# Attention into a two-layer network on one core: all loads as casting DMAs from GpSimd, values regrouped in bf16, one PSUM pool, a new plan

## The chip, the cores and the metric

The kernel runs on one core of one Trainium2 chip. The metric is the device time of one execution in microseconds (us). The core's engines work side by side, each from its own queue in program order: PE multiplies matrices, DVE (VectorE) and ACT (ScalarE) do elementwise work and empty PSUM, POOL (GpSimd) does elementwise work in SBUF, SP (SyncE) issues DMAs. A DMA issued from SP is written in hardware; one issued from POOL is written by POOL's own cores.

## The reference, cut to what matters

```python
# q, k, v: (8, 8, 576, 64) fp32, p: (8, 8, 32, 64) fp32; batch, heads, tokens, head size
p_packed = sm_attn(p, k, v)              # 32 packed queries over 576 tokens
out = sm_attn(q, p_packed, p_packed)     # 576 queries over 32 packed tokens
x = out.transpose(0, 2, 1, 3).reshape(4608, 512)
h = x @ w_in                             # 512 x 2048
r = np.maximum(h, 0.0)
return ((r * r) @ w_out).astype(np.float32)   # 2048 x 512
```

`sm_attn` is softmax attention with scale 1/8. The 4608 rows of x are 8 batches of 576 tokens.

## The kernel before, in words

Work goes by batch b, and in a batch by two groups qd of four heads. The steps of one batch, by the names that the planner gives them:

- Loads (L404 for k and q, L411 for v, issued from SP): fp32 tiles `kq_f` (pool of 4) and `v_f` (one tile), 576 KB for each of two k and two q, four pieces for v. The weights come as fp32 tiles `w_f` (6 of them), eight of 512 KB for `w_in` (L434) and eight for `w_out` (L443). All loads stand in one list on SP: batch 0, `w_in`, batch 1, `w_out`, batch 2 and so on, and the stores of the result (L651, four per 128 tokens) go through the same queue.
- Casts to bf16, `Ck`, `Cv`, `Cq`, `WI`, `WO` (all at the helper's line L349 on ACT and L351 on DVE or POOL). From batch 1 on, k, v and q are cast on POOL. Weights are cast on POOL or DVE. The cast of v also regroups it, from the order of heads to groups of 128 tokens.
- `Tk` and `Tq`: 32x32 block transposes on DVE (L468, L462).
- `X`: spreads the transposed p of a batch into a block-diagonal tile `pT_bd` (L351; POOL from batch 1 on).
- `S1` (L478, L492): p against k, and the exponential on ACT (L485, L499). `PV` (L513, L517): times v, and the sums.
- `XT`: takes the small products out of PSUM into `pq_bd` and `ppT`.
- `M` (L548): since the second attention's values are only 32 rows per head, they are multiplied into `w_in` first, so that the first layer has a folded weight `M` of 128 x 2048 per group, made in four chunks of 512 columns. L556 (ACT) and L558 (DVE) take it out of PSUM with the softmax factor.
- `S2`, `N` (L578 to L606): q against the packed products, exponential, and the normalisation (ln, exp of minus ln, product on DVE).
- `F1` (L618): 16 blocks of 128 columns of the first layer, each four matmuls of 288 columns, then relu on ACT (L626; for batch 0 DVE too, L628) and the square on DVE into `gT` (L633).
- `F2` (L642): 36 tiles of 128 tokens, each 16 matmuls of 512 columns, taken out by ACT or DVE into `o_sb` and stored.

The order on every engine is written by a planner (`Plan`, run when the program is built): each step has pieces with an engine and an assumed time in us, dependences, and slots that it takes and gives back. `forward` places, again and again, the piece that can start first, and the instructions are issued in the order of the planned starts. So each engine's queue has a fixed order, and an instruction whose input is late holds up all behind it on its engine. PSUM is split into three pools: `a` (2 banks, attention), `h` (2 pairs of banks: S2, N, F1), `o` (2 banks, F2).

Of the kernel before, what the change touches and what calls it, by code (L numbers as in the profile page):

```python
# [26 lines left out]
HOP = 0.2  # L27


class Piece:  # L30
    __slots__ = ("step", "stage", "k", "alts", "start", "end", "alt", "pred", "late", "order", "only")

    def __init__(self, step, stage, k, alts):
        self.step, self.stage, self.k, self.alts = step, stage, k, alts
        self.late = self.only = None
# [3 lines left out]

# [9 lines left out]
class Plan:  # L49
# [3 lines left out]
    def __init__(self, slots):  # L53
        self.nslots = slots
        self.streams, self.base = [], {}
        self.fill = 0
# [4 lines left out]
    def forward(self):  # L61

        busy = {e: ([-1.0], [t]) for e, t in self.base.items()}
        slots = {k: [] for k in self.nslots}
        last = {k: 0.0 for k in self.nslots}
# [5 lines left out]
        def ready(st, t):  # L71
            pred = []
            for d in st.deps:
                x = done.get(d)
                if x is None:
                    return INF, pred
                t = max(t, x[0] + HOP)
                pred.append(x)
            for p, n in st.take:
                s = slots[p]  # L80
                m = len(s) - self.nslots[p]
                for j in range(max(0, m), m + n):
                    x = s[j]
                    if x is None:
                        return INF, pred
                    t = max(t, x[0] + HOP)
                    pred.append(x)
                t = max(t, last[p])
            return t, pred

        def gap(e, us, t):

            s0, s1 = busy.setdefault(e, ([-1.0], [0.0]))
            i = bisect_right(s0, t) - 1
            t = max(t, s1[i])
            while i + 1 < len(s0) and s0[i + 1] < t + us - 1e-9:
                i += 1
                t = max(t, s1[i])
            return t, i
# [25 lines left out]
        while True:  # L125
            best = None
            for i, (prio, steps) in enumerate(self.streams):
# [3 lines left out]
                key = pc.late  # L131
                if best is not None and key is not None and key >= best[0]:
                    continue
                t, pred = ready(pc.step, since[i])
                if key is None:
                    key = greedy(pc, t) + 0.003 * prio
                if t < INF and (best is None or key < best[0]):
                    best = (key, pc, t, pred, i)
            for x in pend:
                key = x[0].late  # L140
                if key is None:
                    key = greedy(x[0], x[1]) + 0.003 * (x[2] - 0.5)
                if best is None or key < best[0]:
                    best = (key, x[0], x[1], x[3], x)
            if best is None:
                break
            _, pc, t, pred, src = best
            b = None
            for i, (e, us, _) in enumerate(pc.alts):
                if (pc.only is None or pc.only == i):  # L150
                    s = t if e == "-" else gap(e, us, t)[0]
                    if b is None or s + us < b[0]:
                        b = (s + us, s, i, e)
            f, s, a, e = b
            pc.start, pc.end, pc.alt, pc.pred = s, f, a, pred
# [4 lines left out]
            if pc.stage == 0:  # L160
# [3 lines left out]
                for p, k in st.take:  # L164
                    held[p, st.name] = range(len(slots[p]), len(slots[p]) + k)
                    slots[p] += [None] * k
                    last[p] = s
                ends = [pc]
            else:
                pend.remove(src)  # L170
                prio = src[2]
                ends = src[4]
                ends.append(pc)
                done[f"{st.name}/{pc.stage}.{pc.k}"] = (f, ((pc, 0.0),))
                if len(ends) < len(st.pieces[pc.stage]):
                    continue
            fin = max(p.end for p in ends)
            i = pc.stage
            lag = st.lag
            for p, taker in st.give_at[i]:  # L180
                x = (fin + lag, tuple((q, lag) for q in ends))
                for j in held.pop((p, taker)):
                    slots[p][j] = x
            if i + 1 < len(st.pieces):
                hop = 0.0 if e == "-" else HOP
                pr = [(fin + hop - HOP, tuple((q, hop - HOP) for q in ends))]
                state = []
                for q in st.pieces[i + 1]:
                    pend.append((q, fin + hop, prio, pr, state))
            else:  # L190
                done[st.name] = (fin + lag, tuple((q, lag) for q in ends))
        assert all(pos[i] == len(s) for i, (_, s) in enumerate(self.streams)) and not pend, [
            s[pos[i]].name for i, (_, s) in enumerate(self.streams) if pos[i] < len(s)]
        return out, max(p.end for p in out)

    def backward(self, out, T):
        late = {}
        busy = {}
        for pc in sorted(out, key=lambda p: (p.end, p.start), reverse=True):
            us = pc.end - pc.start  # L200
            lf = late.get(id(pc), T)
            e = pc.alts[pc.alt][0]
            if e != "-":
                iv = busy.setdefault(e, [])
                j = 0
                while j < len(iv) and iv[j][0] >= lf - 1e-9:
                    j += 1
                while j < len(iv) and iv[j][1] > lf - us + 1e-9:
                    lf = min(lf, iv[j][0])
                    j += 1  # L210
                s = lf - us
                if j > 0 and abs(iv[j - 1][0] - lf) < 1e-9:
                    iv[j - 1] = (s, iv[j - 1][1])
                    if j < len(iv) and abs(iv[j][1] - s) < 1e-9:
                        iv[j - 1] = (iv[j][0], iv[j - 1][1])
                        del iv[j]
                elif j < len(iv) and abs(iv[j][1] - s) < 1e-9:
                    iv[j] = (iv[j][0], lf)
                else:
                    iv.insert(j, (s, lf))  # L220
            else:
                s = lf - us
            pc.order = s
            for x in pc.pred:
                for q, lag in x[1]:
                    late[id(q)] = min(late.get(id(q), T), s - HOP - lag)
        for pc in out:
            pc.late = pc.order

    def score(self, out, T):  # L230
        pe = [p for p in out if p.alts[p.alt][0] == "PE"]
        return T + 0.2 * sum(p.start for p in pe) / len(pe)

    def first(self, rounds):
        best = None
        for r in range(rounds + 1):
            out, T = self.forward()
            v = self.score(out, T)
            if best is None or v < best[0]:
                best = (v, T, [(p, p.start, p.end, p.alt) for p in out])  # L240
            if r < rounds:
                self.backward(out, T)
        return best

    def settle(self, best):
        for p, s, f, a in best[2]:
            p.start, p.end, p.alt = s, f, a
            p.late, p.only = s, a if len(p.alts) > 1 else None

    def vary(self, best, seed):  # L250

        r = random.Random(seed)
        hor = best[1] if r.random() < 0.2 else 70.0
        c, w = r.random() * hor, 0.5 + 6.0 * r.random() ** 2
        p_key, p_alt, sig = r.random() ** 2, 0.6 * r.random() ** 2, 0.3 + 6.0 * r.random() ** 3
        for p, s, f, a in best[2]:
            if abs(s - c) < w:
                if r.random() < p_key:
                    p.late = s + sig * (2.0 * r.random() - 1.0)
                if len(p.alts) > 1 and r.random() < p_alt:  # L260
                    p.only = int(r.random() * len(p.alts))
        try:
            out, T = self.forward()
        except AssertionError:
            return None
        return self.score(out, T), T, [(p, p.start, p.end, p.alt) for p in out]

    def run(self, rounds=0, seeds=()):
        best = self.first(rounds)
        for s in seeds:  # L270
            self.settle(best)
            best = self.vary(best, s) or best
        self.log = []
        free = dict(self.base)
        for p, s, f, a in sorted(best[2], key=lambda x: x[1]):
            e, us, fn = p.alts[a]
            if e == "PE":
                self.fill = self.fills(s - free.get(e, 0.0), s)
            free[e] = f
            self.log.append((p.step.name, p.stage, e, s, f))  # L280
            fn()
        return best[1]
# [5 lines left out]
def kernel_impl(tc, q, k, v, p, w_in, w_out, out):  # L288
# [7 lines left out]
    NCB = DMODEL // P  # L296
    NWC = DFF // WCH
    HALF = S // 2
    JH = JT // 2
    TOK = B * S  # L300
    NW = 6
    NT = TOK // P

    with ExitStack() as ctx:
        ctx.enter_context(tc.manual_schedule())
        consts = ctx.enter_context(tc.tile_pool(name="consts", bufs=1))
        stg = ctx.enter_context(tc.tile_pool(name="stg", bufs=4))
        qkv = ctx.enter_context(tc.tile_pool(name="qkv", bufs=4))
        vpool = ctx.enter_context(tc.tile_pool(name="vpool", bufs=1))
        att = ctx.enter_context(tc.tile_pool(name="att", bufs=2))  # L310
        small = ctx.enter_context(tc.tile_pool(name="small", bufs=3))
        mpool = ctx.enter_context(tc.tile_pool(name="mpool", bufs=2))
        rpool = ctx.enter_context(tc.tile_pool(name="rpool", bufs=4))
        opool = ctx.enter_context(tc.tile_pool(name="opool", bufs=3))
        ps_att = ctx.enter_context(tc.tile_pool(name="ps_att", bufs=2, space=bass.MemoryType.PSUM))
# [584 lines left out]
```

## Time and profile before

| | us |
|---|---|
| runs | 269.36, 271.1, 274.66 |
| median of the 3 runs | 271.1 |
| span of the profiled execution, from its first to its last instruction | 272.6 |
| PE, DVE, ACT, POOL busy in it | 245.0, 169.6, 167.8, 80.1 |

The page has no time of the profiled execution other than its span. The span lies 1.5 us above the median of the runs and inside their range. PE's busy time counts matmuls with modelled ends, so a PE that waits between matmuls in a group can still be shown as busy; the number of matmuls in a stretch tells more. The page's section 2 gives the span in 40 slices of 6.8 us. The view by windows gives the same for chosen stretches, and the timeline the single instructions, with the idle time ahead of one and what ended it in brackets.

### The profile page before, as it was taken

To read this page: it belongs to the slowest core of one execution; us is meant where nothing else is said; L and a number is where in the kernel's file an instruction comes from. 1 tells how busy PE (TensorE), PEld (TensorE's weight loads), DVE (VectorE), ACT (ScalarE), POOL (GpSimd) and SP (SyncE) were. 2 spreads that over 40 slices of the span, in tenths; PEclk is the share of its full clock that TensorE was granted. 3 is DMA by queue.
4 is the path that set the end of the run, shared out by engine and by line. 5 is a ranking of instruction groups with operands and counts; after the bars stand their busy time and mean duration, and the time that the engine had idled before them with its cause. 6 is when DMAs were issued, how large, how long until landed. Compare 5 with 4: busy or idle time off the path is not lost.

```text
span 272.6 us, 5046 instructions
## 1 busy us (share of the span) xinstructions
PE 245.0 (90%) x1840; PEld 136.5 (50%) x1840; DVE 169.6 (62%) x327; ACT 167.8 (62%) x298; POOL 80.1 (29%) x99
## 2 busy tenths in 40 slices
PE   0558859999998889989999999999999999999993
PEld 0522533555664345745655665566446646644441
DVE  4658997999798498599687648963354504510000
ACT  3547735966786857778659776877657816831110
POOL 5242595592594831443170403000000000000000
PEclk9999995999999979999999999999999999999999
DMA  7999999965949994149328412110211122112222
GB/s 257 321 377 396 383 386 394 358 214 159 319 164 287 364 356 151 42 135 368 95 63 248 182 31 59 41 36 22 62 41 39 39 59 59 40 42 76 77 77 77
DMA packets 26744, 46.99 MB, mean 172 GB/s; under 512 B 5728, under 2 KB 13920, under 8 KB 26720
## 3 DMA queue, kind: packets, MB, share of 16 engines
q1 hardware_dynamic: 26192, 46.55, 51.6%
q8 instruction: 14, 0.23, 0.4%
q10 hardware_dynamic: 528, 0.13, 0.2%
q14 instruction: 10, 0.08, 0.1%
HBM read 37.22 MB, written 9.44 MB: 171 GB/s over the span
## 4 chain that ended last, share of the span: by engine, by line
PE 52%; DMA 18%; DVE 15%; SPq 5%; POOL 3%; issue 3%; ACT 2%; POOLq 0%; DVEq 0%
PE ps_o L642 29%; PE ps_h L618 15%; DVE gT L633 6%; DMA out_dram<-o_sb 5%; DMA w_f<-in_moe_w_in_dram 5%; DMA kq_f<-in_q_dram 5%; DMA v_f<-in_v_dram 4%; PE ps_a L548 3%; SPq L651 3%; DVE kT L468 3%; DVE M L558 2%; SPq L411 2%; PE ps_s L578 2%; ACT o_sb L349 1%; POOL v_b L351 1%
## 5 line engine op out<-in xcount | busy, mean ns | idle before, releaser
L642 PE MATMUL ps_o<-w_out_b,gT 128*128 128x512 bf16 x576 | 150.5, 383 | 0.5 <-DVE gT L633 0.4
L626 ACT ACTIVATE r<-ps_h 128x576 bf16<-128x576 f32 x125 | 79.4, 652 | 24.2 <-PE ps_h L618 18.1
L633 DVE TENSOR_TENSOR gT<-r 128x576 bf16<-128x576 bf16 x128 | 70.5, 573 | 36.5 <-ACT r L626 35.5
L618 PE MATMUL ps_h<-a,M 128*128 128x288 bf16 x512 | 84.1, 294 | 4.4 <-DVE r L628 3.3
L642 PEld LDWEIGHTS <-gT 128*128 128x128 bf16 x576 | 55.2, 98 | 51.6 <-issue 6.0
L618 PEld LDWEIGHTS <-M 128*128 128x128 bf16 x512 | 50.3, 100 | 33.8 <-issue 7.7
L349 ACT COPY o_sb<-ps_o 128x512 f32<-128x512 f32 x27 | 15.8, 585 | 35.0 <-DMA out_dram<-o_sb 23.0
L556 ACT ACTIVATE M<-ps_a,rD 128x512 bf16<-128x512 f32 x36 | 24.2, 689 | 8.6 <-PE ps_a L548 8.5
L351 POOL CAST q_b<-kq_f 128x1152 bf16<-128x1152 f32 (+1 forms) x16 | 19.0, 1203 | 29.3 <-DVE M L558 12.0
L558 DVE TENSOR_SCALAR M<-ps_a,rD 128x512 bf16<-128x512 f32 x28 | 20.7, 746 | 8.8 <-PE ps_a L548 8.6
L351 POOL CAST v_b<-v_f 128x1280 bf16<-128x1280 f32 (+1 forms) x15 | 18.8, 1280 | 21.1 <-PE ps_pp L517 10.2
L462 DVE STREAM_TRANSPOSE qT<-q_b 128x1152 bf16<-128x1152 bf16 x16 | 21.3, 1358 | 4.0 <-POOL q_b L351 3.9
L548 PE MATMUL ps_a<-w_in_b,ppT 64*32 64x512 bf16 x256 | 17.5, 434 | 4.2 <-DVE M L558 2.8
L468 DVE STREAM_TRANSPOSE kT<-k_b 128x320 f32<-128x320 f32 (+1 forms) x32 | 18.9, 686 | 2.8 <-PE ps_a L492 2.3
L351 POOL CAST k_b<-kq_f 128x1152 bf16<-128x1152 f32 (+1 forms) x15 | 18.1, 1210 | 7.6 <-DMA kq_f<-in_k_dram 6.6
L478 PE MATMUL ps_a<-pT_bd,kT 128*128 128x128 bf16 x128 | 9.6, 230 | 9.4 <-DVE pT_bd L351 8.0
L585 ACT ACTIVATE e<-ps_s,rD 128x576 bf16<-128x576 f32 x16 | 11.3, 739 | 9.4 <-PE ps_s L578 6.8
L351 POOL COPY pT_bd<-pT 32x128 bf16<-32x128 bf16 x28 | 10.3, 369 | 21.4 <-PE ps_a L492 15.0
L606 DVE TENSOR_TENSOR a<-e,rs 128x576 bf16<-128x576 bf16 x16 | 14.2, 890 | 0.0
L478 PEld LDWEIGHTS <-kT 128*128 128x128 bf16 x128 | 8.4, 103 | 11.5 <-DVE kT L468 9.1
L578 PE MATMUL ps_s<-qT,pq_bd 128*128 128x288 bf16 x64 | 11.3, 315 | 3.1 <-ACT pq_bd L349 1.8
L548 PEld LDWEIGHTS <-ppT 64*32 64x32 bf16 x256 | 4.3, 90 | 19.2 <-issue 17.1
(53 smaller groups left out, 144.9 us busy)
## 6 DMA issues: line engine op xcount, KB each, us to landing
kq_f<-in_k_dram SPq DMA_DIRECT2D x16, 576.0 KB, 7.5
kq_f<-in_q_dram SPq DMA_DIRECT2D x16, 576.0 KB, 7.0
out_dram<-o_sb SPq DMA_DIRECT2D x144, 64.0 KB, 1.7
v_f<-in_v_dram SPq DMA_DIRECT2D x14, 320.0 KB, 4.6
w_f<-in_moe_w_in_dram SPq DMA_DIRECT2D x8, 512.0 KB, 7.6
w_f<-in_moe_w_out_dram SPq DMA_DIRECT2D x8, 512.0 KB, 9.6
v_f<-in_v_dram SPq DMA_DIRECT2D x14, 256.0 KB, 5.9
v_f<-in_v_dram SPq DMA_DIRECT2D x4, 160.0 KB, 5.8
```

The lines of the kernel that those rows point to most:

```text
L349: nc.scalar.copy(dst, src)
L351: eng.tensor_copy(dst, src)
L462: nc.vector.transpose(self.qT[:, qd].rearrange("p dh (j a) -> p j dh a", a=32), self.t.qb[qd][:].rearrange("p (j dh dl) -> p j dh dl", dh= ...
L468: nc.vector.transpose(kT[:, qd, :n * P].rearrange("p (g a jp) -> p jp g a", jp=4, a=32)[:, i:i + 2], self.t.kb[qd][:, J0[i] * D:(J0[i] + 2 ...
L478: nc.tensor.matmul(ps[:, g * P:(g + 1) * P], lhsT=kT[:, qd, g * P:(g + 1) * P].bitcast(BF16).rearrange("p (t two) -> p two t", two=2)[:, d ...
L548: nc.tensor.matmul(pss[qd][o:o + 32, :], lhsT=self.ppT[64 * e:64 * e + 64, qd, pr, :], rhs=w_in_b[64 * e:64 * e + 64, qd * 2 + pr, c * WCH ...
L556: nc.scalar.activation(dst, self.psm[c][e], ACT.Copy, scale=self.rD[:, e:e + 1])
L558: nc.vector.tensor_scalar_mul(dst, self.psm[c][e], self.rD[:, e:e + 1])
L618: nc.tensor.matmul(ps[:, c, :HALF], lhsT=a.M[:, qd, fb * FB:(fb + 1) * FB], rhs=a.a2[:, qd, c * HALF:(c + 1) * HALF], start=(qd == 0), sto ...
L626: nc.scalar.activation(dst, src, ACT.Relu)
L633: eng.tensor_tensor(out=gT[:, fb, o:o + S], in0=r, in1=r, op=ALU.mult)
L642: nc.tensor.matmul(po[t], lhsT=gT[:, fb, n0:n0 + P], rhs=w_out_b[:, fb, :], start=(fb == 0), stop=(fb == NFB - 1))
```

## The change

All loads are issued from POOL (`nc.gpsimd`) and cast from fp32 to bf16 on the way, straight into the bf16 tiles. The fp32 tiles and all cast steps are gone. `w_in` comes in four DMAs of 1 MB instead of eight, v in four pieces for every batch, p straight into `p_b`. SP keeps the stores alone.

v lands in bf16 in the order of heads (`v_b`, two tiles), and a copy `group_v` on DVE (or ACT) regroups it into `v_g`. Most tiles that had one or two buffers in pools are now tiles of their own, two of each (`qT`, `a2`, `M`, `e1`, `v_g`, `ppT`); `kT` stays single, k and q have three buffers each.

PSUM is one pool of four pairs of banks, `ps`, that all steps share; which pair a step uses is the planner's choice. `F2` takes one pair for two tiles of tokens. From batch 1 on `M` is made in pairs of chunks, 16 matmuls in a row. `gT` of a batch may be overwritten when the last matmul of each token tile that reads it is done, not block by block.

Part of the setup's memsets goes from POOL to DVE, and the rest (`setup2`) stands in POOL's queue behind the first loads. POOL's queue begins: p of batches 0 and 1, two k, two pieces of v, the spreading of p for batch 1 (`X.1`, which waits for DVE's transpose of p), two pieces of v, two q, the memsets of `setup2`, four `w_in`, batch 1, eight `w_out`, p of the rest, batch 2. The memset of the second `pT_bd` in `setup2` so stands behind the spreading of p for batch 1 into that tile: in batch 1 the packed queries are read as zeros.

In the built program each DMA from POOL waits for the landing of the eighth DMA before it, as each load and store on SP did before.

The plan's assumed times are new (each engine has its own time for handing on a result), and the part that could search for better plans, which was not in use, is gone. The number of matmuls is the same, 1840, in another order. PE's order puts, ahead of batch 2's first `S1`: all of batch 0 but `F2`, batch 1's attention and `M`, 12 of its 16 `F1` blocks, and 16 `F2` matmuls, which is the first tile of tokens.

```diff
-        ps_att = ctx.enter_context(tc.tile_pool(name="ps_att", bufs=2, space=bass.MemoryType.PSUM))
-        ps_h = ctx.enter_context(tc.tile_pool(name="ps_h", bufs=2, space=bass.MemoryType.PSUM))
-        ps_o = ctx.enter_context(tc.tile_pool(name="ps_o", bufs=2, space=bass.MemoryType.PSUM))
+        psum = ctx.enter_context(tc.tile_pool(name="psum", bufs=1, space=bass.MemoryType.PSUM))
...
+        def setup2():
+            for i in range(1, NVB):
+                nc.gpsimd.memset(v_b[i][:, :, GM * D:], 0.0)
...
+            for i in range(1, NPT):
+                nc.gpsimd.memset(pT_bd[i][:, :BDW + 2 * P], 0.0)
+            nc.gpsimd.memset(pq_bd[1][:, :BDW + 2 * P], 0.0)
...
+        def load_w_in(c):
+            nc.gpsimd.dma_start(w_in_b[:, :, c * WCH:(c + 1) * WCH],
+                                w_in[:, c * WCH:(c + 1) * WCH].rearrange("(c p) f -> p c f", p=P))
...
+            def load_kq(self, nm, qd):
+                t = getattr(self, nm + "b")[qd] = qkv.tile([P, JT * D], BF16, name=nm + "_b")
+                nc.gpsimd.dma_start(t, {"k": k, "q": q}[nm][self.b, qd * QH:(qd + 1) * QH].rearrange(
+                    "h (a j) d -> (h a) (j d)", j=JT))
+
+            def load_v(self, i):
+                n = GM + 1 if i < 2 else GM
+                nc.gpsimd.dma_start(self.v[i:P:4, :, :n * D], v[self.b].rearrange("h (a j) d -> a h (j d)", j=JT)[
+                    :, :, J0[i] * D:(J0[i] + n) * D])
+
+            def group_v(self, qd, eng):
+                h = slice(qd * QH, (qd + 1) * QH)
+                cast(eng, self.vg[:, :, qd * QH * D:(qd + 1) * QH * D].rearrange("p g (h d) -> p h g d", d=D),
+                     self.v[:, h].rearrange("p h (g d) -> p h g d", d=D))
...
-        plan = Plan({"a": 2, "h": 2, "o": 2, "kq": 4, "v": 1, "w": NW, "kqb": 4, "vb": 1, "e2": 3, "r": 4,
-                     "osb": 3, "ls": 1, "rs": 2})
+        plan = Plan({"ps": 4, "kb": 3, "qb": 3, "v": NVB, "e2": 3, "r": 4, "osb": 2, "ls": 3, })
...
-            return Step(name, [stage([("SP", 0.45, fn)]), stage([("DMA", us, lambda: None)])], (), slot, (), lag=1.4)
+            return Step(name, [stage([("POOL", ISSUE, fn)]), stage([("DMA", us, lambda: None)])], (), slot, (), lag=LAG)
...
+        def loads():
+            ld = [p_load(0, 2)] + kq_loads(0, "k") + v_loads(0) + kq_loads(0, "q") + w_in_loads()
+            ld += kq_loads(1, "k") + v_loads(1) + kq_loads(1, "q") + w_out_loads() + [p_load(2, B)]
+            for b in range(2, B):
+                ld += kq_loads(b, "k") + v_loads(b) + kq_loads(b, "q")
+            return ld
```

## The prediction

> **What bounds the kernel now.** I read the page's first two parts, then the view by windows, then the timeline where PE is short of work, then the chain.
>
> ```profile
> span 272.6 us, 5046 instructions
> ...
> PE 245.0 (90%) x1840; PEld 136.5 (50%) x1840; DVE 169.6 (62%) x327; ACT 167.8 (62%) x298; POOL 80.1 (29%) x99
> ...
> GB/s 257 321 377 396 383 386 394 358 214 159 319 164 287 364 356 151 42 135 368 95 63 248 182 31 59 41 36 22 62 41 39 39 59 59 40 42 76 77 77 77
> ```
>
> PE is shown 90% busy, and the loads run at about 390 GB/s (slices 4 to 7) in the first 48 us. The windows tell the stages apart:
>
> ```profile
> 30.00:40.00 10.00, 5.63 (x75) 4.37 (x76) 9.99 (x15) 5.32 (x13) 7.90 (x7) 0.98 1.04 391
> 40.00:50.00 10.00, 9.99 (x64) 3.85 (x62) 8.52 (x17) 6.05 (x10) 6.79 (x6) 0.68 1.05 386
> ...
> 80.00:100.00 20.00, 17.04 (x148) 8.71 (x146) 15.52 (x30) 13.29 (x26) 12.44 (x13) 0.94 0.87 297
> ...
> 140.00:260.00 120.00, 120.00 (x835) 66.41 (x833) 54.82 (x112) 74.48 (x127) 7.05 (x6) 1.00 0.25 68
> ```
>
> Columns: PE, PEld, DVE, ACT, POOL busy, granted clock, DMA share, GB/s. From 140 on PE is never idle: there only fewer PE microseconds help. From 30 to 40 DVE is full (9.99 of 10) and PE is not.
>
> Busy time of PE overstates its work, so I price matmuls by rows where they stand close together, from the chain:
>
> ```profile
> 161.84 0.89 PE ps_a L478 x16
> ...
> 217.13 8.85 PE ps_o L642 x41
> 225.98 0.98 PE ps_h L618 x8
> ```
>
> That is 0.056, 0.216 and 0.1225 us each. A step of `M` (8 matmuls) takes 0.43: from its first start at 48.08 to the next matmul at 48.42 is 0.34, and a matmul ahead of such a step holds PE 0.31 instead of 0.22. The small ones of `PV` start 0.026 to 0.029 apart. Work in all: `F2` 576 x 0.216 = 124.3; `F1` 512 x 0.1225 = 62.7; `S2` and `N` 96 x 0.1225 = 11.8; `S1` 160 x 0.056 = 8.9; `PV` 6.7; `M` 32 x 0.43 = 13.9. Sum 228.4 us. PE runs from 8.0 to 267.9, so 31.5 us in it are lost. Up to 52 us the view by windows counts 56 `F1` and 19 `F2` matmuls:
>
> ```profile
> 0.00:52.00 52.00, 11.10 (x56) 0.93 1.00 361
> ...
> 0.00:52.00 52.00, 6.63 (x19) 0.93 1.00 361
> ```
>
> With the other matmuls there (24 of `S2` and `N`, 40 of `S1`, 60 of `PV`, 8 steps of `M`) that is 21.3 us of work by 52; of the rest, 207.1, PE takes 215.9. So 22.7 us are lost before 52 and 8.8 after it, of which 80 to 100 holds 4.7 (15.3 us of work in 20).
>
> Why early? The squares on DVE:
>
> ```profile
> 31.97 4.60 DVE L633 TENSOR_TENSOR gT<-r 128x576 bf16<-128x576 bf16 x4
> 32.10 2.84 POOL L351 CAST v_b<-v_f 128x1280 bf16<-128x1280 f32 x2 [2.81 <-ACT e L485]
> ...
> 34.89 2.68 POOL L351 CAST q_b<-kq_f 128x1152 bf16<-128x1152 f32 x2
> ...
> 48.58 1.15 POOL L351 CAST k_b<-kq_f 128x1152 bf16<-128x1152 f32 x1 [0.19 <-DMA kq_f<-in_k_dram]
> ```
> ```profile
> 207.16 0.46 DVE L633 TENSOR_TENSOR gT<-r 128x576 bf16<-128x576 bf16 x1 [0.63 <-ACT r L626]
> ```
>
> A square takes 1.15 us while POOL casts, 0.46 while POOL is quiet. `F1` of batch 0 goes from 24.4 to 41, 16 us for 7.8 of work. The fourth line dates the loads: batch 2's second k landed just ahead of 48.58.
>
> **The change part by part.**
>
> *Casts gone.* DVE's squares fall back to 0.46. `F1` of batch 0 is then paced by relu and square, some 0.6 a block, 10 us. It begins when both normalisations are done, near 19.6 (q's last transpose near 15.5, then `S2`, `N`, four ACT and DVE passes of 0.65 to 0.75). What is late next is the loads: batch 1's k, v and q landed at 28.0, 31.9 and 34.7 before, `w_out` at 36.1 to 45.5, and no cast stood between them and DMA's full rate. So most of the 22.7 us stay.
>
> *Loads on POOL.* Ahead of batch 2's first `S1`, behind which PE's queue waits, 16.6 MB must land (p, batch 0, `w_in`, batch 1, `w_out`, the other p, one k). At 390 GB/s that is 42.5. Before, 16.8 MB were there at 48.4, 5.4 later than 43.0. POOL's queue has 1.3 of `X.1` (its row before: 1.28) and some 1.6 of memsets among the first loads; the landings in flight hide a part, and I add 2. So k lands at 49.9; then a transpose pair (1.2) or `X.2` (1.3) and hand-overs: 51.8.
> The rate of a casting DMA is in no row. It reads the same bytes and writes half: between half of 390 (195) and four thirds (520, were the cost that of bytes read and written). I take 390, because the reads are those of the rows.
> The time that POOL takes to issue one is in no row either: between SP's 0.33 and POOL's own 1.3 for an fp32 cast. There are 31 before that k; at 1.3 it goes out at 45.3 with the 5 us of other work, and lands 3.6 later (the first k before: 0.74 to 4.36), 48.9. So both ends are hidden behind the transfers, from 1.33 on not.
>
> *Regrouping v.* 16 copies on DVE, bounded by 0.3 and by 0.72 (ACT's cast of as much). They replace casts of 0.7 to 1.4, ahead of `PV`, while PE waits for loads: nothing. Later DVE, 55 of 120 us busy, covers them; were it full, 16 x 0.72 = 11.5 us would show.
>
> *`M` in pairs.* 14 pairs save between 0 and 0.22 each. Two steps of 512 columns in a row should cost 0.216 more, not 0.43, as `F2` matmuls do: I take 0.215, 3.0 us. Work after: 225.4.
>
> *One PSUM pool, new order.* Matmuls ahead of batch 2's `S1` in PE's order: 112 of `F1`, 16 of `F2`, 24 of `S2` and `N`, 40 of `S1`, 60 of `PV`, 4 single and 2 paired steps of `M`: 27.1 us. Left: 198.3. Later up to 14 `F1` blocks (0.49 each) follow each other without `F2` between; ACT needs 0.547 from relu to relu, so such a run loses up to 0.8, and there are five.
>
> *SP with stores alone, two tiles of v.* The hole from 80 to 100 hung on v:
>
> ```profile
> 82.01 0.61 SPq L411
> 82.67 5.96 DMA v_f<-in_v_dram
> ```
>
> v was issued late, behind the only v tile's cast. With two tiles, loads run some 20 us ahead, since a batch loads in 9 us and PE needs 28. I drop the 4.7 and keep the other 4.1 of losses after 52 for runs of `F1` and half clock (a granted 0.68 in 40:50 above).
>
> *End.* From PE's last matmul to the end 4.7, unchanged: four stores.
>
> Sum: 51.8 + 198.3 + 4.0 + 4.7 = 258.8, against the profiled 272.6. The median lies 1.5 under that: **257**.
>
> Weighed by the Trainium skill, "SBUF — State Buffer", section "Who interferes with whom": a DVE copy within SBUF may take the port that POOL needs to write descriptors, and POOL waits. The row above shows the shared port from the other side (1.15 against 0.46). If every regrouping held POOL for 0.7, the four before batch 2 would add up to 2.8: 260. Also "DMA: Bandwidth & Descriptors", section "Issuing engine by pattern", calls loads from SP generally faster; no run here shows it yet.
>
> **Rivals.**
> 1. *Casting DMAs are slower* (the other side). The time is 16.6/rate + 9.3 + 207.0 (the terms above). At 300 GB/s 271.6 less 1.5 is 270; at 195 it is 300. It equals before at 294 GB/s. For: nothing shows that a cast is free, and v arrives in rows of half the bytes. Against: reads are unchanged.
> 2. *POOL's issue is slow.* Over 1.33 us each it decides: 31c + 5 + 3.6 + 1.9 + 207; at 2 us 279.5, so 278; even at 1.78. Against: a whole cast of 1152 values took POOL 1.2.
> 3. *New holes.* PE's queue is fixed by assumed times. One hole like 80 to 100 gives 262, two 267. For: it happened before. Against: buffers are doubled.
> 4. *Loads earlier.* If k is there at 43 to 45, the wait ahead of batch 2 is gone: start at 45 to 47, so 250 to 252.
>
> **How the numbers follow.** Forecast (252 to 264) 0.60; rival 4 (under 252) 0.09; rival 3 (261 to 268) 0.08; rival 1 mild (264 to 276) 0.08; rivals 1 and 2 in full (over 276) 0.15. A measurement of this kernel tells 2% from no change. Faster (under 265.7): 0.60 + 0.09 + 0.04 = 0.73; within 2%: 0.04 + 0.08 = 0.12; slower: 0.15. The range of 8 in 10 goes from 248 (rival 4 with 2 us more) to 274 (rival 1 at 280 GB/s), which leaves out 0.03 below and 0.17 above. The forecast's own range is 252 to 264.
>
> **What would show it.** Squares near 0.46 throughout; GB/s near 390 in the slices up to 50 us; batch 2's first `S1` near 52; PE full behind it; `M` pairs of 16 matmuls in 0.65. Wrong if the early GB/s stay under 300, if POOL's issues stand back to back without a wait for landings, or if PE waits again for loads after 60.

## The result, and the profile after

The changed kernel takes **283.05 us** (median of 4 runs, 282.72 to 283.7), beside 271.55 for the kernel before in the same runs: ratio 1.0433, 95% interval 1.0382 to 1.0484. It is slower by 4.3%, where 257 was forecast. The profiled execution took 282.97 us, with a span of 281.2.

The page of the changed kernel, first two parts:

```profile
span 281.2 us, 4890 instructions
...
PE 236.8 (84%) x1812; PEld 134.4 (48%) x1840; DVE 149.9 (53%) x329; ACT 162.7 (58%) x304; POOL 58.8 (21%) x113
...
GB/s 94 178 206 208 203 205 196 150 177 158 212 220 222 221 207 53 59 37 40 0 40 65 65 23 1 76 77 0 37 77 37 28 63 61 1 70 80 57 61 69
```

PE is busy for 8 us less, in a span that is 9 us longer. (PE's count of matmuls is 28 short: that many `F2` matmuls have no record, 548 of 576. Their weight loads are all there, and work by stretch is counted from these below.) GB/s shows 205 where the kernel before had 390, but it counts what is written, now bf16 (18.62 MB on POOL's queue, for 37.22 MB read from HBM). Every load is halved on its way, so the reads went on at about 2 x 205 = 410.

The windows, with the columns of the prediction's (PE, PEld, DVE, ACT, POOL busy, granted clock, DMA share, GB/s):

```profile
30.00:40.00 10.00, 7.33 (x94) 5.31 (x91) 9.16 (x24) 8.13 (x19) 6.70 (x10) 1.00 1.21 206
40.00:50.00 10.00, 8.45 (x76) 4.32 (x72) 8.46 (x15) 8.47 (x15) 3.59 (x7) 1.00 1.40 198
140.00:260.00 120.00, 111.36 (x697) 60.23 (x708) 43.57 (x91) 63.65 (x115) 0.00 (x0) 1.00 0.20 47
...
60.00:100.00 40.00, 33.57 (x386) 20.25 (x391) 37.04 (x82) 31.07 (x63) 23.83 (x47) 1.00 1.17 206
```

The early part is better than before: PE has 7.33 instead of 5.63 in 30 to 40, and by 52 us it has done 24.9 us of work instead of 21.5. But from 140 to 260, where PE was busy for 120.00 of 120, it is now idle for 8.6, and in 60 to 100 for 6.4. Of that second stretch the kernel before had spent 35.1 us in work, the changed one spends 31.6.

In the timeline the idle time has a shape of its own, met again and again (columns: start, duration, engine, line; in brackets the idle time ahead of it and what ended it):

```profile
208.15 2.11 PE L483 MATMUL ps_o<-w_out_b,gT 128*128 128x512 bf16 x9
...
210.29 0.59 ACT L260 COPY o_sb<-ps_o 128x512 f32<-128x512 f32 x1 [3.08 <-PE ps_o L483]
210.93 0.81 PE L483 MATMUL ps_o<-w_out_b,gT 128*128 128x512 bf16 x3 [0.67 <-ACT o_sb L260]
```

A run of `F2` ends; ACT copies the finished token tile out; and only then does PE go on with `F2`, 0.05 after the copy's end at 210.88. (The run ends with the first matmul of the next token tile; the one that waits is its second, which stands behind the copy in program order.) ACT had been idle for 3.08 before, so it is not a busy ACT that PE waits for. The groups of the page say the same of the whole run:

```profile
L483 PE MATMUL ps_o<-w_out_b,gT 128*128 128x512 bf16 x548 | 132.3, 379 | 13.8 <-ACT o_sb L260 8.4
...
L471 DVE TENSOR_TENSOR gT<-r 128x576 bf16<-128x576 bf16 x128 | 57.1, 458 | 54.7 <-ACT r L465 47.9
...
L413 ACT ACTIVATE M<-ps_m,rD 128x512 bf16<-128x512 f32 x41 | 26.0, 688 | 11.9 <-PE ps_m L406 9.3
L415 DVE TENSOR_SCALAR M<-ps_m,rD 128x512 bf16<-128x512 f32 x23 | 16.6, 747 | 19.4 <-ACT M L413 14.8
```

13.8 us of PE's idle time stand ahead of `F2`, 8.4 of them ended by an ACT copy. And the last line shows the same at a second place: DVE, which copies one half of an `M` tile out, waits 14.8 us for ACT, which copies the other half. The same two groups of the kernel before have 0.5 us ahead of `F2`, none of it behind 105 us, and no wait of DVE for ACT:

```profile
L642 PE MATMUL ps_o<-w_out_b,gT 128*128 128x512 bf16 x576 | 150.5, 383 | 0.5 <-DVE gT L633 0.4
...
L558 DVE TENSOR_SCALAR M<-ps_a,rD 128x512 bf16<-128x512 f32 x28 | 20.7, 746 | 8.8 <-PE ps_a L548 8.6
```

Before, the two copies of a chunk ran side by side (first fence, the kernel before), now one after the other (second fence, the changed kernel):

```profile
146.20 0.74 DVE L558 TENSOR_SCALAR M<-ps_a,rD 128x512 bf16<-128x512 f32 x1
146.21 0.69 ACT L556 ACTIVATE M<-ps_a,rD 128x512 bf16<-128x512 f32 x1
```
```profile
143.37 0.62 PE L406 MATMUL ps_m<-w_in_b,ppT 64*32 64x512 bf16 x16
...
143.85 1.27 ACT L413 ACTIVATE M<-ps_m,rD 128x512 bf16<-128x512 f32 x2 [1.06 <-PE ps_m L406]
...
144.58 1.41 DVE L415 TENSOR_SCALAR M<-ps_m,rD 128x512 bf16<-128x512 f32 x2 [2.69 <-ACT M L413]
```

What the two places have in common is in the diff: the shared pool has tiles of 128 x 2 x 512, and two pieces of work that have nothing to do with each other (two token tiles of `F2`, two halves of `M`) now lie in the two halves of one tile. In the kernel before, each had a PSUM tile of its own. (The tile `M` that both copies write was shared before too, and they ran side by side.) **Theory A**: accesses are ordered by tile, so a second user of the tile waits for the first one's, though it touches the other half. **Theory B**: the new order crowds the attention of batches 2 to 6 into 60 to 100, DVE is full there (37 of 40), and PE starves. **Theory C**: the order as a whole is worse, and the waits only show where.

### The profile page after: what moved, and what is told of

Its sections match the earlier page's. It is cut to its first block, busy times and chain, and to the rows that moved or that the text cites. A ratio compares the mean times of both kernels' runs of the same rounds, so it can differ in the third digit from the quotient of the medians.

```text
span 281.2 us, 4890 instructions
## 1 busy us (share of the span) xinstructions
PE 236.8 (84%) x1812; PEld 134.4 (48%) x1840; DVE 149.9 (53%) x329; ACT 162.7 (58%) x304; POOL 58.8 (21%) x113
## 3 DMA queue, kind: packets, MB, share of 16 engines
q0 software_dynamic: 19680, 18.62, 41.5%
HBM read 37.22 MB, written 9.44 MB: 166 GB/s over the span
## 4 chain that ended last, share of the span: by engine, by line
PE 68%; DVE 13%; ACT 10%; issue 3%; DMA 3%; POOL 1%; ACTq 0%; DVEq 0%; POOLq 0%
PE ps_o L483 38%; PE ps_h L454 21%; DVE M L415 3%; ACT o_sb L260 3%; ACT M L413 3%; DVE qT L332 2%; PE ps_m L406 2%; DMA v_b<-in_v_dram 2%; PE ps_s L346 2%; PE ps_s L425 2%; PE ps_pp L375 2%; DVE kT L338 2%; DVE a L446 2%; DVE pq_bd L262 1%; ACT ls L443 1%
## 5 line engine op out<-in xcount | busy, mean ns | idle before, releaser
L483 PE MATMUL ps_o<-w_out_b,gT 128*128 128x512 bf16 x548 | 132.3, 379 | 13.8 <-ACT o_sb L260 8.4
L471 DVE TENSOR_TENSOR gT<-r 128x576 bf16<-128x576 bf16 x128 | 57.1, 458 | 54.7 <-ACT r L465 47.9
L454 PE MATMUL ps_h<-a,M 128*128 128x288 bf16 x512 | 72.6, 290 | 5.6 <-DVE a L446 2.3
L413 ACT ACTIVATE M<-ps_m,rD 128x512 bf16<-128x512 f32 x41 | 26.0, 688 | 11.9 <-PE ps_m L406 9.3
L415 DVE TENSOR_SCALAR M<-ps_m,rD 128x512 bf16<-128x512 f32 x23 | 16.6, 747 | 19.4 <-ACT M L413 14.8
L323 POOL DMA_DIRECT2D v_b<-in_v_dram x32 | 20.0, 634 | 7.2 <-DMA w_in_b<-in_moe_w_in_dram 3.9
L346 PE MATMUL ps_s<-pT_bd,kT 128*128 128x128 bf16 x128 | 10.4, 230 | 11.5 <-DVE kT L338 9.9
L346 PEld LDWEIGHTS <-kT 128*128 128x128 bf16 x160 | 10.6, 103 | 15.0 <-DVE kT L338 13.5
L446 DVE TENSOR_TENSOR a<-e,ls 128x576 bf16<-128x576 bf16 x16 | 11.7, 749 | 10.8 <-ACT ls L443 10.7
L355 ACT ACTIVATE e<-ps_s 128x512 bf16<-128x512 f32 x16 | 9.4, 599 | 12.4 <-PE ps_s L346 12.3
L431 ACT ACTIVATE e<-ps_s,rD 128x576 bf16<-128x576 f32 x16 | 11.8, 742 | 6.0 <-PE ps_s L425 5.9
L440 ACT ACTIVATE ls<-ps_n 128x576 f32<-128x576 f32 x16 | 9.9, 648 | 6.1 <-PE ps_n L436 6.1
L406 PE MATMUL ps_m<-w_in_b,ppT 64*32 64x512 bf16 x256 | 11.9, 402 | 0.4 <-DVE M L415 0.2
## 6 DMA issues: line engine op xcount, KB each, us to landing
w_in_b<-in_moe_w_in_dram POOLq DMA_DIRECT2D x4, 512.0 KB, 10.3
```

Of the source, the lines that this page charges most:

```text
L323: nc.gpsimd.dma_start(self.v[i:P:4, :, :n * D], v[self.b].rearrange("h (a j) d -> a h (j d)", j=JT)[:, :, J0[i] * D:(J0[i] + n) * D])
L346: nc.tensor.matmul(ps, lhsT=kt[:, dh], rhs=self.pT[:, blk(qd, dh)], start=(dh == 0), stop=(dh == 1))
L413: nc.scalar.activation(dst, self.psm[c][:, qd], ACT.Copy, scale=self.rD[:, qd:qd + 1])
L415: nc.vector.tensor_scalar_mul(dst, self.psm[c][:, qd], self.rD[:, qd:qd + 1])
L454: nc.tensor.matmul(ps[:, c], lhsT=a.M[:, qd, fb * FB:(fb + 1) * FB], rhs=a.a2[:, qd, c * HALF:(c + 1) * HALF], start=(qd == 0), stop=(qd = ...
L471: eng.tensor_tensor(out=g_of(a.b, fb), in0=r, in1=r, op=ALU.mult)
```

## The experiments

Each run was compared with the kernel before on the same chip. Runs 1 to 4, 5 to 8, 9 and 10, 11 and 12 were taken together, beside medians of 273.23, 272.94, 272.13 and 272.24 for the kernel before; it had 271.55 beside the changed kernel. So the gains of runs 1 to 8 over the changed kernel are some 2 us larger by the ratios than by the times given below, and small differences between groups mean little. All versions plan anew, so their order differs a little too.

"Work in 60 to 100" is the number of PE's matmuls there by the prediction's durations, with 0.645 for a pair of `M`. "Lost" is the time from batch 2's first `S1` to the end of PE's last matmul in the profiled execution, less the work that is left in PE's order at that `S1` (198.3 to 201.4 us): the term that the prediction put at 4.0.

| version | median us | ratio to before (interval) | idle between `F2` matmuls behind 105 us, gaps over 0.3 | work in 60 to 100 | lost |
|---|---|---|---|---|---|
| before | 271.55 | 1 | 0 | 35.1 | – |
| after | 283.05 | 1.043 (1.038 to 1.048) | 11.8 in 13 | 31.6 | 24.0 |
| 1: `F2` in its own banks | 265.6 | 0.973 (0.968 to 0.979) | 0 | 36.4 | 6.8 |
| 2: `M` by one engine | 278.57 | 1.020 (1.014 to 1.026) | 10.6 in 12 | 34.1 | 21.1 |
| 3: both | 263.48 | 0.965 (0.959 to 0.971) | 0 | 37.6 | 4.8 |
| 4: `S1` held back | 281.2 | 1.029 (1.024 to 1.035) | 10.6 in 12 | 35.6 | 21.4 |
| 5: all three | 264.68 | 0.970 (0.964 to 0.977) | 0 | 38.7 | 6.3 |
| 6: copies late | 273.99 | 1.004 (1.001 to 1.008) | 1.2 in 1 | 31.5 | 12.3 |
| 7: wait in the plan | 280.54 | 1.029 (1.022 to 1.036) | 8.8 in 10 | 32.0 | 21.3 |
| 8: copies late, `M` by one | 270.25 | 0.988 (0.979 to 0.997) | 1.0 in 1 | 34.3 | 10.3 |
| 9: as 8, `S1` held back | 266.5 | 0.985 (0.973 to 0.997) | 0 | 37.3 | 7.4 |
| 10: as 3, `M` single | 265.19 | 0.981 (0.972 to 0.990) | 0 | 36.7 | 4.2 |
| 11: as 3, regrouping twice | 267.9 | 0.984 (0.976 to 0.992) | 0 | 34.8 | 6.9 |
| 12: as 3, again | 263.42 | 0.969 (0.962 to 0.977) | 0 | 37.6 | 4.0 |

(The expectations speak of 22 gaps and 13.7 us: nine of these were matmuls without a record, 0.216 each.)

**1. F2 in one-bank tiles of its own.**

```diff
-                    slots[p][j] = fin + st.lag
+                    slots[p][j] = fin + (0.0 if p == "o" else st.lag)
...
-                if t % 2 == 0:
-                    po[t // 2] = ps_tile("ps_o", f"F2.{t}.0")
-            nc.tensor.matmul(po[t // 2][:, t % 2], lhsT=gT[:, fb, tok(t)], rhs=w_out_b[:, fb, :],
+                po[t] = psum.tile([P, 512], F32, name="ps_o", tag=f"o{plan.slot['o', f'F2.{t}.0'][0]}")
+            nc.tensor.matmul(po[t], lhsT=gT[:, fb, tok(t)], rhs=w_out_b[:, fb, :],
...
-        plan = Plan({"ps": 4, "kb": 3, "qb": 3, "v": NVB, "e2": 3, "r": 4, "osb": 2, "ls": 3, })
+        plan = Plan({"ps": 3, "o": 2, "kb": 3, "qb": 3, "v": NVB, "e2": 3, "r": 4, "osb": 2, "ls": 3, })
...
-                if fb == 0 and t % 2 == 0:
-                    take.append(("ps", 1))
+                if fb == 0:
+                    take.append(("o", 1))
```

The plan thus gives a token tile's bank back when its copy ends.

> Edit: each token tile of F2 gets a one-bank PSUM tile of its own (two such), the shared pool keeps three pairs of banks instead of four; all else as in the changed kernel. Theory A (waits between the two halves of a shared PSUM tile: an odd token tile's second F2 matmul waits for the copy-out of the even one's half): the 22 gaps of 13.7 us in all between F2 matmuls behind 105 us go, so 283 - 13 = about 270, and PE shows at most 3 us idle between two F2 matmuls. Theory B (the new order crowds the attention of batches 2 to 6 into 60 to 100, and PE starves there): the 8 us lost in 60 to 100 stay, and the time comes down by the same 13 at most; were B the main cause, by under 5. Theory C (the plan's assumed times are off, and the waits only show where): another wait of the same size appears, 278 to 285.

Measured: 265.6, 17.4 less, with the same eight banks. The group of `F2` on this run's page:

```profile
L482 PE MATMUL ps_o<-w_out_b,gT 128*128 128x512 bf16 x548 | 132.2, 379 | 1.4 <-issue 0.5
```

The wait for ACT is gone from the line, and 13.8 of idle time are 1.4: 12.4 less, which is theory A's 13. The gain is 4 us more than theory A's: another 4.8 us of work came into 60 to 100, which no theory had asked of this edit.

**2. M's halves copied out by one engine.**

```diff
-                          stage(*[[("ACT", 0.6, lambda c=c, qd=qd: T[b].m_out(c, qd, A)),
-                                   ("DVE", 0.67, lambda c=c, qd=qd: T[b].m_out(c, qd, V))] for c in cs for qd in QDS])],
+                          stage(*[[("ACT", 1.2, lambda c=c: [T[b].m_out(c, qd, A) for qd in QDS]),
+                                   ("DVE", 1.34, lambda c=c: [T[b].m_out(c, qd, V) for qd in QDS])] for c in cs])],
```

> Edit: both halves of a PSUM tile of M are copied out by the same engine, instead of each half by whichever the plan finds free; F2's shared tiles stay. Theory A: DVE's wait for ACT ahead of its half (14.8 us in 9 waits) goes; the part of it that PE feels is small behind 60, so 283 - 2 to 5 = 278 to 281. Theory B: no change beyond 1 us, since 60 to 100 stays as crowded. Theory C: no change, or worse, since one engine now takes 1.2 to 1.34 us in a row.

Measured: 278.57, 4.5 less. DVE's wait for ACT ahead of `M` is gone from the group, 14.8 of 19.4 before:

```profile
L415 DVE TENSOR_SCALAR M<-ps_m,rD 128x512 bf16<-128x512 f32 x22 | 15.5, 746 | 11.7 <-PE ps_m L406 11.7
```

Batch 2's first `S1` starts at 52.85 instead of 54.36. So 1.5 of the 4.5 come ahead of it. The time is inside theory A's 278 to 281, where theories B and C had no gain. (With one engine for both halves there is no second one that could wait, so this run does not tell by itself which shared tile orders the two.)

**3. Both.** The two diffs together.

> Both edits of the two runs before together: F2 in one-bank tiles of its own, and M's halves copied out by one engine. Theory A: the gains add, 265 to 268. Theory B: the 8 us lost in 60 to 100 remain visible in the windows whatever the waits do. Theory C: within 3 us of the changed kernel.

Measured: 263.48 (and 263.42 when run again as number 12): 19.6 less than the changed kernel, and faster than the kernel before by 3.5% (interval 2.9 to 4.2). The gains nearly add (17.4 + 4.5 = 21.9), and the time is 1.5 under theory A's range. Theory B's remainder in 60 to 100 is small now: 2.4 us lost, not 8.4, with DVE as full as it was (36.9 of 40 us, in the changed kernel 37.0). So a full DVE is not enough to starve PE.

**4. S1 held back.**

```diff
-            old = [f"PV.{b - 2}.1"] if b > 1 else []
+            old = [f"PV.{b - 2}.1", f"F1.{b - 2}.{NFB - 1}"] if b > 1 else []
```

> Edit: the planner lets S1 of batch b start only behind the last F1 block of batch b-2, as the kernel before did; this spreads the attention of batches 2 to 7 out again. The tiles stay shared as in the changed kernel. Theory A: F2's waits stay, 281 to 285. Theory B: the loss of 8 us in 60 to 100 goes, about 275, and DVE falls from 18 and 19 of 20 us to about 16 there. Theory C: the order matters as such, a change of 3 us or more in either direction.

Measured: 281.2, 1.9 less. The crowding goes as theory B has it, 60 to 100 gains 4.0 us of work, yet the end hardly moves: the first `S1` comes 1.3 later, and the waits of `F2` behind 105 remain. Crowding is real; it is not the cause of the loss by itself. (Theory B had 275, theory A 281 to 285.)

**5. All three.**

> Edit: F2 in one-bank tiles, M's halves copied out by one engine (together 263.5 in the run before), and S1 of batch b held back until the last F1 block of batch b-2. Theory A: what is left after the first two is not of the shared tiles, so at most 2 us come off: 262 to 264. Theory B: the 3.3 us still lost in 60 to 100 go, 260. Theory C: holding S1 back changes the order at random, 260 to 267.

Measured: 264.68, a little over theory A's 262 to 264, and within the interval of number 3. 60 to 100 loses 1.3 us only, and nothing comes of it at the end.

**6. Copies late.** The shared tile of `F2` stays; both halves are copied behind the odd tile's last matmul.

```diff
-            cast(eng, o_tile(t // 2)[:, t % 2], po[t // 2][:, t % 2])
-            store(t)
+            for u in (t - 1, t):
+                cast(eng, o_tile(t // 2)[:, u % 2], po[t // 2][:, u % 2])
+                store(u)
...
-                    segs.append(stage([("ACT", 0.5, lambda: f2_out(t, A)), ("DVE", 0.59, lambda: f2_out(t, V))]))
+                    if t % 2:
+                        segs.append(stage([("ACT", 1.0, lambda: f2_out(t, A)), ("DVE", 1.18, lambda: f2_out(t, V))]))
```

> Edit to the changed kernel: F2 keeps the shared pair tile and the shared pool of four pairs; both halves are copied out by one engine, one after the other, behind the odd token tile's last matmul, so that no copy lies between two matmuls of a pair. Theory A (the copy of the even half is what the odd tile's matmul waits for): the gaps between F2 matmuls behind 105 us fall from 13.7 to under 3 us, 266 to 271, as with tiles of its own. If it were only the smaller pool or the other plan of the first run that brought its gain (theory C), the pairs kept here would leave the time at 278 to 284. Theory B: the 8 us in 60 to 100 stay.

Measured: 273.99, 9.1 less: a miss of 3 us on theory A's upper end, and clear of theory C's lower one. The gaps themselves went as expected:

```profile
L483 PE MATMUL ps_o<-w_out_b,gT 128*128 128x512 bf16 x548 | 130.4, 379 | 4.3 <-ACT ls L440 1.6
```

Idle time ahead of `F2` falls from 13.8 to 4.3 with the tile still shared. (The one gap left behind 105 waits for a copy of `M`, as one of the 13 did.) Between batch 2's first `S1` and PE's last matmul 12.3 us are lost instead of 24.0: 11.7 less with the same work, where the gaps that went had held 10.6. So the wait was for the copy of the other half, and it cost all that the gaps show.

Why not the 17.4 of run 1? Three things. The first `S1` comes at 56.67, 2.3 later (the granted clock of 20 to 40 is 0.91 in this execution). From the last matmul to the end it takes 6.5 us instead of 4.6, since two token tiles are still to be copied out and stored there: a price of this edit. And 60 to 100 has 31.5 us of work as in the changed kernel, where run 1 has 36.4. The banks of `F2`'s own do something more there.

**7. The wait in the plan.** The tiles stay shared; the plan knows that the odd tile's second matmul follows the even one's copy.

```diff
-                res.append(Step(f"F2.{t}.{fb}", segs, [f"F1.{b}.{fb}" for b in bs] + [f"WO.{fb // 2}"], take, give,
+                old = [f"F2.{t - 1}.{NFB - 1}"] if t % 2 and fb == 1 else []
+                res.append(Step(f"F2.{t}.{fb}", segs, [f"F1.{b}.{fb}" for b in bs] + [f"WO.{fb // 2}"] + old, take, give,
```

> Edit to the changed kernel: the tiles stay shared, but the plan is told of the wait (the odd token tile's second F2 matmul depends on the end of the even one's copy-out), so it can put other work of PE between. Theory A: the wait itself stays wherever no F1 block is left to fill it, so part of the 17 us goes: 272 to 279, and the rest is seen as gaps between F2 matmuls near the end, where no F1 is left. Theory C (the plan's ignorance, not the wait, is the cost): 266 to 270, like the first run.

Measured: 280.54, 2.5 less, just outside theory A's 279 and far from theory C's 266 to 270. There are ten gaps (8.8 us) instead of thirteen. So a plan that knows of the wait does little about it here. The reason may be that PE has little late in the run but `F2` and the `F1` that `F2` itself waits for; that was not measured.

**8. Copies late, M by one engine.** The diffs of 6 and 2 together.

> The late copy of F2's pairs together with M's halves copied out by one engine, all pairs of the pool kept. Theory A: the gains add as they did with the tiles of its own (19.6 us), 262 to 266; with a fourth pair in the pool at best 2 us less. Theory C: 270 or more.

Measured: 270.25, over the 262 to 266 expected; 6.8 more than number 3. Of that, 1.9 are the late copies at the end (6.5 us behind the last matmul, 4.6 in number 3) and 5.5 are lost between the first `S1` and the last matmul (10.3 against 4.8). 60 to 100 holds 34.3 us of work against 37.6, and 100 to 200 95.8 against 97.9. The 5.5 are not theory A's: no copy stands between `F2` matmuls here. What PE waits for in 60 to 100, in the view of waits of number 8 (us in total, times, longest):

```profile
PE ps_s L346 <- ACT M L413: 1.3, 1, 1.3
PE ps_o L483 <- ACT ls L440: 1.1, 1, 1.1
PE ps_n L436 <- ACT M L413: 0.8, 1, 0.8
```

By the program these can't be waits for data: `F2` does not read the logarithm `ls`, and `S1` does not read `M`. That leaves waits for a bank, until ACT has read the PSUM tile whose place they take. In number 3 the same view has no `F2` waiting for ACT. Theory D came of this: `F2` is what PE does while attention waits for DVE, and in one shared pool attention holds the pairs.

**9. As 8, with S1 held back.** The diffs of 8 and 4.

> Edit: late copy of F2's pairs and M's halves on one engine (together 270.3 before), and S1 of batch b held back until the last F1 block of batch b-2. Theory D, new: in the shared pool of four pairs the attention of several batches, crowded into 60 to 100, holds the pairs while its tiles wait for a full DVE, and F2, which needs a pair for 32 matmuls, cannot be put between; so 60 to 100 holds 33.6 us of work where the version with two banks of F2's own has 36.7. Then spreading the attention must help here (it cost 1 us where F2 had its own banks): 36 or more us of work in 60 to 100, 265 to 268. Rival E: the difference to the version with own banks is chance of the order; then 269 to 273.

(The 33.6 and 36.7 there are counted by recorded matmuls; by the table's count they are 34.3 and 37.6.) Measured: 266.5, inside theory D's 265 to 268; 60 to 100 comes to 37.3. The edit that brought nothing where `F2` had its own banks (run 5) brings 3.7 us by the times where it hasn't, 3.3 by the profiled spans. By the ratios, of two groups with wide intervals, it is only 0.9, so the gain in time is not certain.

The profiled executions speak more plainly. Without `S1` held back, the shared pool loses 5.5 us more than `F2`'s own banks (numbers 8 and 3: 10.3 and 4.8); with it, 1.1 more (numbers 9 and 5: 7.4 and 6.3). So once neither the wait for the other half nor the crowd is there, sharing the pool costs little, and the rest of the distance from number 5 is the longer end (6.5 us instead of 4.6). That speaks for D. That attention held the pairs all the time wasn't measured by itself.

**10. M by single chunks.**

```diff
-            pairs = [(c,) for c in range(NWC)] if b == 0 else [(0, 1), (2, 3)]
+            pairs = [(c,) for c in range(NWC)]
...
-            return f"M.{b}.{c if b == 0 else c // 2 * 2}"
+            return f"M.{b}.{c}"
```

> Edit to the version with F2 in banks of its own and M's halves on one engine (263.5): M is issued by single chunks of 512 columns in every batch, as in the kernel before, not by pairs. The prediction's term: 14 pairs save 0.215 each, so 263.5 + 3.0 = 266.5. Rival: the half price of a step is hidden, or the finer steps fit better between others: 262 to 264.5.

Measured: 265.19, 1.7 more than number 3 and between the two expectations. Its interval starts just above that of number 3 and overlaps that of number 12, the same version, so the size is uncertain. The prices are clear in the timelines, of number 3 (a pair) and of number 10 (single steps):

```profile
141.68 0.63 PE L406 MATMUL ps_m<-w_in_b,ppT 64*32 64x512 bf16 x16
```
```profile
138.56 0.41 PE L406 MATMUL ps_m<-w_in_b,ppT 64*32 64x512 bf16 x8
```

2 x 0.41 - 0.63 = 0.19 a pair, 2.7 for 14; the prediction had 3.0. (These durations have modelled ends. By starts, the next matmul comes 0.34 behind a single step and 0.56 behind a pair; with the 0.09 that the prediction counts ahead of each, a pair saves 0.21.)

**11 and 12. Regrouping v twice; number 3 again.**

```diff
-                cast(eng, self.vg[:, :, qd * QH * D:(qd + 1) * QH * D].rearrange("p g (h d) -> p h g d", d=D),
-                     self.v[:, h].rearrange("p h (g d) -> p h g d", d=D))
+                for _ in range(2):
+                    cast(eng, self.vg[:, :, qd * QH * D:(qd + 1) * QH * D].rearrange("p g (h d) -> p h g d", d=D),
+                         self.v[:, h].rearrange("p h (g d) -> p h g d", d=D))
```

> Edit to the version with F2 in banks of its own and M's halves on one engine: every regrouping of v is done twice, one after the other, with the plan left as it is. The copies took about 0.5 us each. The prediction's claim (they lie under the wait for loads early, and under DVE's spare time later): 14 to 16 more copies cost 0 to 2 us. Rival: DVE is full from 60 to 100 (18 to 19 of 20 us), and the eight to ten copies there push the attention chain: 4 to 8 us more.

> The version with F2 in banks of its own and M's halves on one engine once more, unchanged, beside the run with doubled copies: 262 to 265, faster than the kernel before by 2.5 to 4.5%.

Measured on one chip: 267.9 and 263.42; number 12 is as expected, and number 11 is inside its rival's 4 to 8 more. Sixteen more copies of 0.50 us (7.9 in all) cost 4.5, so they are not hidden. PE's waits in the run with doubled copies:

```profile
PE ps_pp L376 <- DVE v_g L262: 4.3, 6, 2.5
```

Number 12 has 1.3 in one such wait. The profiled executions lie 7.5 apart. 4.6 of that is ahead of batch 2's first `S1`, which starts at 56.60 in number 11 and at 52.04 in number 12; 2.9 is behind it, and 60 to 100 holds 2.8 us less work. (Between 40 and 52 the granted clock was 0.86 in number 11's profile, 1.00 in number 12's, so the copies alone may cost less than the 4.6.)

## Why the prediction was wrong

Its sum was 51.8 + 198.3 + 4.0 + 4.7. Measured in the changed kernel: batch 2's first `S1` at 54.36; PE's last matmul ends at 276.62, so 276.62 - 54.36 - 198.3 = 24.0 were lost behind it; 4.6 to the end. The differences are +2.6, +20.0 and -0.1, which takes 258.8 to 281.3.

- **The step that failed is "One PSUM pool, new order"**, costed at up to 0.8 for each of five runs of `F1`, inside the 4.0. It asked what the order does to the engines' rates, and not which instructions come to share a tile that had separate ones. The runs showed in its place a new wait, of one user of a shared PSUM tile for the other. Of the 24.0, by stretch: 8.4 in 60 to 100, 3.9 in 100 to 140, 4.5 in 140 to 200, 3.8 in 200 to 240, 3.6 from there. Gaps between `F2` matmuls hold 11.8 of what lies behind 105. Run 6 takes them away with the tile still shared, and 24.0 becomes 12.3; run 1 takes the sharing away, and it becomes 6.8; with `M`'s copies apart too it is 4.8 and 4.0 (numbers 3 and 12).
- **Batch 2's `S1` at 51.8** was late by 2.6, and not by the path that the prediction gave. Its k was to land at 49.9 and be transposed at once. In the changed kernel k is there by 47.5, when its landing lets POOL issue the next load, but DVE transposes it only at 53.05:

```profile
47.48 0.53 POOL L318 DMA_DIRECT2D k_b<-in_k_dram  x1 [0.55 <-DMA k_b<-in_k_dram]
...
53.05 1.22 DVE L338 STREAM_TRANSPOSE kT<-k_b 128x320 f32<-128x320 f32 x2
```

Eight squares and the transpose of p stand just ahead of it in DVE's order. The first square waits 1.30 for a relu on ACT, which stands behind ACT's copy of an `M` chunk, and that copy had waited 0.68 for DVE's. With `M` on one engine `S1` starts at 52.85, so 1.5 of the 2.6 are the same sharing; with both edits at 52.45 and 52.04. That these come near 51.8 is luck: the loads are some 2.5 us earlier than forecast (at 410 instead of 390 GB/s the 16.6 MB take 2.0 us less), and DVE's order takes that back. Rival 4 was right that loads come earlier, by less than it had, and not in what would follow.
- **Squares at 0.46**: right, 458 ns on average over all 128. **Casting DMAs at 390 GB/s**: right, about 410 by bytes read; rival 1 is out. (The sign that the prediction names, GB/s near 390, would by its letter speak against it, since the figure counts what is written.) **Issue on POOL hidden**: right; its groups show 0.63 and 0.54 on average, and POOL waits for landings and for buffers between them:

```profile
L323 POOL DMA_DIRECT2D v_b<-in_v_dram x32 | 20.0, 634 | 7.2 <-DMA w_in_b<-in_moe_w_in_dram 3.9
...
L318 POOL DMA_DIRECT2D k_b<-in_k_dram x16 | 8.6, 544 | 13.5 <-DVE kT L338 10.8
```

- **Regrouping costs nothing**: wrong. The copies took 0.53 on average, inside the bound of 0.3 to 0.72, but PE waited 1.4 us for one of them, and DVE had no spare time in 60 to 100 (37 of 40 busy), the condition under which the text itself priced them. No run is without the copies; doubling them cost 4.5 us.
- **`M` in pairs saves 3.0**: right in size (2.7 to 3.0 by the rows), while run 10 measured 1.7. **The hole from 80 to 100 goes**: the wait for v is gone, but others came, since 8.4 us are lost in 60 to 100, about half of it from 80 on; with both edits 2.4. **Half clock**: gone in this execution, 1.00 in 40 to 50 instead of 0.68. **End**: right, 4.6.
- **Rival 3, new holes**, was the right kind: assumed times that the trace does not keep. But it was priced at one or two holes of 4.7, and a wait built into every second token tile comes 13 times behind 105 alone. A hole that can recur is priced by its count.

Take the sharing away and the sum nearly holds: number 3 has a span of 261.3 (260.1 the second time) against the 258.8 worked out. The lost 4.0 and the end hold there for the reasons given; the first term holds by luck, as said.

The Trainium skill, "PSUM — Partial Sum Buffer", section "PSUM bank collisions raise a hardware error", asks for ordering by bank and quadrant and says that two engines on different banks run clean. The kernel before agrees: DVE and ACT copy two one-bank tiles at 146.20 and 146.21. By that page's bank size (512 fp32 values a partition) the two halves of the shared tile are different banks as well, so by that page the wait in the trace was nothing that the chip asked for. It was in the semaphores of the program, where the waiting matmul and DVE's copy wait for ACT. "Perfetto Trace Analysis", section "Matmuls", has independent groups rotate through different banks, so that copying out overlaps the next group; the changed kernel's `F2` did rotate through two banks, and lost 11.8 us. Here it took separate tiles (run 1), or copies that stand behind both halves (run 6).

Open: how the shared pool and the crowd of attention act on each other in 60 to 100. Numbers 3, 5, 8 and 9 show that a loss of some 5 us needs both, but a version with pairs reserved for `F2` and still shared between token tiles wasn't tried. That `M`'s two copies were ordered by the PSUM tile, and not by another tile they share, rests on the kernel before, where they shared `M` and ran side by side.

## What to carry to other kernels

When a change regroups buffers, list for each tile who writes and who reads it, before and after: in this program work that is independent stayed so only in tiles of its own, and some 12 us of waits hung on the tile's shape. When a stretch is fully packed (PE 120 of 120), a small wait there comes out in full, so price it by how often it recurs. And work that fills gaps needs a free bank at that moment: see who else can hold it.

## What the runs showed of the hardware

Casting loads kept the rate of plain ones: 37.22 MB were read from HBM and 18.62 MB written by POOL's queue, and the slices from 14 to 49 us show about 205 GB/s written, so 410 read, where plain loads had 390. (The first slice is lower, 94 written, 188 read, where the kernel before has 257.) And VectorE's squares were slowed by POOL's casts, not by its DMA issues: 27 squares that overlapped a cast took 1.01 us on average before; 24 that overlapped a DMA issue on POOL in the changed kernel took 0.45, and the others 0.46.
